# Nine fillers between the M units, w_in's last quarter scaled in one step, six bias additions moved to VectorE

## The chip, the cores and the metric

The program runs on one core of one Trainium2 chip. The core has five engines with instruction streams of their own: TensorE (PE: matmuls, with its weight loads as PEld), VectorE (DVE), ScalarE (ACT), GpSimd (POOL) and SyncE (SP, which here only issues transfers). They meet through semaphores. Matmul results land in PSUM; the other tiles lie in SBUF; large tensors and two scratch arrays lie in DRAM. The metric is the time of one execution on the device in microseconds (us), smaller is better. The kernel before takes 903.31 us, the median of three runs (903.01 to 904.61).

## The reference

Two stages follow each other. The first is a spectral filter over the sequence axis of x, with 8 batches of 3008 positions and 256 channels:

```python
X = np.fft.rfft(x, axis=1);  Xr, Xi = X.real, X.imag
Yr = Xr @ w_r - Xi @ w_i + b_r
Yi = Xr @ w_i + Xi @ w_r + b_i
Yr = np.sign(Yr) * np.maximum(np.abs(Yr) - 0.01, 0.0)   # Yi likewise
y = np.fft.irfft(Yr + 1j * Yi, n=3008, axis=1)
```

The second is a feed-forward layer on all 24064 rows of y, with 2048 hidden features and an ELU between two matrix products:

```python
h = y @ w_in
g = np.where(h > 0.0, h, np.exp(np.minimum(h, 0.0)) - 1.0)
out = g @ w_out
```

## The kernel before

**The transform as matmuls.** 3008 is 47 x 64, so the transform and its inverse are each split into two small ones, and a batch passes through five kinds of units, each a handful of matmuls with one eviction out of PSUM:

- A (`unit_A`, six per batch): 64-point transform of x. ScalarE evicts to the tile A, and pairs of units are stored to the DRAM scratch DA (line 172).
- X (`unit_X`, eight): 47-point transform. Its operand Z is DA read back with another axis on the partitions (`load_Z`, line 181, two transfers). Result: XT.
- M (`unit_M`, twelve): the complex product with the weights, the bias and the soft threshold for 128 frequencies at a time, see below. Result: Y.
- B (`unit_B`, six): first part of the inverse. ScalarE evicts to Bz, and pairs of units are stored to the DRAM scratch DB (line 336).
- Y (`unit_Y`, eight): second part of the inverse. Its operand Bs is DB read back (`load_Bs`, line 344, four transfers). Result: yT, which is the hidden layer's input, transposed.

**The M unit.** The complex product is done with three real products. Xd is the real part minus the imaginary part (GpSimd, line 240, issued two units ahead). One product K = Xd @ w_i goes to one half of the PSUM tile (`kp`), and X_r @ (w_r - w_i) and X_i @ (w_r + w_i) go to the other (`ps[:, 0]`); K added to each gives both parts. VectorE first makes Kb = K + b_r (line 265, 128x256) and then yb = ps + Kb with Kb used for both halves (line 266, 128x512). The imaginary half should have had b_i, so GpSimd adds b_i - b_r (`bias_d`) to that half (line 274, 128x256), then clips (line 275) and subtracts (line 278): the soft threshold.

**The steps.** The feed-forward layer runs in 376 steps, 47 per batch; eight steps make a block of 512 rows, with 256 hidden features per step. `front_mm` (line 789) makes the two halves of the hidden tile `hps` on TensorE. `Elu` then runs over ScalarE, GpSimd or VectorE (lines 803 to 814), and VectorE's mix (line 824) writes `gT`, which also sets the PSUM of `hps` free. `back` (line 844) multiplies by w_out two steps later and adds up in PSUM; after the eighth step the block is evicted (line 855) and stored (line 862).

The transform of the next batch is woven into these steps by hand. `plan(b)` makes a list with one entry per step: while the layer runs on batch b, the steps hold the last Y units of batch b, the X, M, B and first Y units of batch b + 1 (entries ("n", 0) and ("n", 1), called n0 and n1 here), and the A units of batch b + 2. A step holds at most one unit, whose matmuls are issued between the two halves of `front_mm`. Y and A units serve as fillers between the M units; `room` says how many fillers may stand there, `cut` behind which M units, and what is left over stands at the end, behind the last B unit. `f1` holds what is issued late in a step: transfers, the first two Xd, and in the first batch also the weight sums (line 228) and the scaling of w_in.

In a step without an M unit GpSimd does both halves of `Elu.least` (line 812). In a step with an M unit ScalarE does that work in another form, so that GpSimd is free for the M unit's own operations. In the first four steps VectorE does it.

**What sets the order.** Every engine runs its instructions in the order in which the program lists them. All loads and stores of DA, DB, Z, Bs and the outputs are issued by SP in program order, so an instruction of SP that waits for a semaphore holds up those behind it. A unit's PSUM tile has one buffer for all kinds of units (`psF`, line 758), so a unit's matmuls wait until the unit before has been evicted; `hps` has four buffers.

**The last quarter of w_in.** w_in arrives in four quarters and is scaled by 2/3008 into bfloat16 (`scale_w_in`, lines 736 and 738). The last quarter feeds the steps with features 1536 to 2047, of which step 6 is the first; VectorE scales its two halves in steps 4 and 5 of the first batch:

```python
f1[4].append((scale_w_in, (3, True, 0)))
f1[5].append((scale_w_in, (3, True, 1)))
```

Of the kernel before, what the change touches and what calls it, by code (L numbers as in the profile page):

```python
# [8 lines left out]
ALU = mybir.AluOpType  # L9
AF = mybir.ActivationFunctionType  # L10
BF16 = mybir.dt.bfloat16
F32 = mybir.dt.float32
# [13 lines left out]
def kernel(  # L26
# [11 lines left out]
    nc = tc.nc  # L38
    P = nc.NUM_PARTITIONS

    B, S, D = x.shape
# [20 lines left out]
    bias_bc = constp.tile([P, 2 * D], F32, name="bias_bc")  # L62
    bias_d = constp.tile([P, D], F32, name="bias_d")
# [13 lines left out]
    wk1 = ctx.enter_context(tc.tile_pool(name="wk1", bufs=1))  # L77
# [39 lines left out]
    def unit_ps(name, alone):  # L117
        if alone:
            return pre2.tile([P, 2, 512], F32, name=name, tag="pre2")
        return psF.tile([P, 2, 512], F32, name=name, tag="fps")  # L120
# [9 lines left out]
    def later(alone, f):  # L130
        if alone:
            f()
        else:
            after.append(f)
# [99 lines left out]
    def unit_D(b, k):  # L234

        if k >= NJ // 2:
            return
        Xd_of[b, k] = wk3.tile([P, 2, P], BF16, name="Xd", tag="Xd")
        XT, o = XT_of[b], k * P
        nc.gpsimd.tensor_tensor(  # L240
            Xd_of[b, k][:], XT[:, :, 0, o : o + P], XT[:, :, 1, o : o + P], ALU.subtract
        )

    def unit_M(b, q, i):

        k = 2 * q + i
        XT, Xd, o = XT_of[b], Xd_of.pop((b, k)), k * P
        ps = unit_ps("mps", False)
        kp = ps[:, 1, 0:D]
        for lhs, rhs, dst in (  # L250
            (lambda dt: Xd[:, dt], lambda dt: wcat_r[:, dt, D : 2 * D], kp),
            (lambda dt: XT[:, dt, 0, o : o + P], lambda dt: wsum[:, 0, dt], ps[:, 0, 0:D]),
            (lambda dt: XT[:, dt, 1, o : o + P], lambda dt: wsum[:, 1, dt], ps[:, 0, D : 2 * D]),
        ):
            for dt in range(2):
                nc.tensor.matmul(dst, lhsT=lhs(dt), rhs=rhs(dt), start=dt == 0, stop=dt == 1)  # L256
        if i == 0:
            Y_of[b, q] = wk3.tile([P, 2, 2 * D], BF16, name="Y", tag="Y")
        yb = wk3.tile([P, 2 * D], F32, name="yb", tag="yb")
        Y_ = Y_of[b, q]  # L260

        def done():
            two = lambda t: t.rearrange("p (c d) -> p c d", c=2)
            Kb = wk1.tile([P, D], F32, name="Kb", tag="Kb")
            nc.vector.tensor_tensor(Kb[:], kp, bias_bc[:, 0:D], ALU.add)  # L265
            nc.vector.tensor_tensor(  # L266
                two(yb[:]), two(ps[:, 0]), Kb[:].unsqueeze(1).to_broadcast([P, 2, D]), ALU.add
            )

        clips = []  # L270

        def clip_():
            clips.append(wk2.tile([P, 2 * D], F32, name="clip", tag="clip"))
            nc.gpsimd.tensor_tensor(yb[:, D : 2 * D], yb[:, D : 2 * D], bias_d[:], ALU.add)  # L274
            nc.gpsimd.tensor_scalar(clips[0][:], yb[:], LAM, -LAM, ALU.min, ALU.max)  # L275

        def sub_():
            nc.gpsimd.tensor_tensor(Y_[:, i, :], yb[:], clips[0][:], ALU.subtract)  # L278

        jobs.append((clip_, lambda: unit_D(b, k + 2), sub_))  # L280
        later(False, done)

    held = []
# [584 lines left out]
    def put(kind, b, *a):  # L868
        return ({"A": unit_A, "X": unit_X, "M": unit_M, "B": unit_B, "Y": unit_Y}[kind], (b, *a))

    def plan(b):

        f0 = [[] for _ in range(PER)]
        f1 = [[] for _ in range(PER)]
        n1, n2 = b + 1, b + 2
        lead = int(b == 0)
        early = 6 if b == 0 else 4
        seq = [("y", u) for u in range(2, early)]
        if b == 0:
            seq.insert(2, ("-",))  # L880
        rest_ = []
        if n1 < B:
            due = 38 + b
            seq += [("X", u) for u in range(8)]
            fill = [("y", u) for u in range(early, 8)]
            if n2 < B:
                fill += [("A", u) for u in range(6)]
            else:
                fill += [("-",)] * 6
            room = max(0, min(10, due - 5 - (b > 0) - lead - len(seq) - 17))  # L890
            fill, rest_ = fill[:room], fill[room:]
            cut = ([-1, 4] if b == 0 else [-1, 11, 0, 4, 8, 2, 6, 10, 1, 11])[: len(fill)]
            fill = fill[::-1]
            seq += [fill.pop() for c in cut if c < 0]
            for k in range(12):
                seq.append(("M", k // 2, k % 2))
                if k % 2 and k > 1:
                    seq.append(("B", k // 2 - 1))
                for c in cut:
                    if c == k:  # L900
                        seq.append(fill.pop())
            if b == 0:
                seq.append(rest_.pop(0))
            seq.append(("B", 5))
            k = due - lead - len(seq)
            seq += rest_[:k] + [("-",)] * (k - len(rest_))
            seq += [("n", 0), ("n", 1)] + rest_[k:]
        else:
            seq += [("y", u) for u in range(early, 8)]
        xs = (14, 18, 22) if b == 0 else (1, 4, 7)  # L910
        for t, u in enumerate(seq, lead):
            if u[0] == "y":
                f0[t].append(put("Y", b, u[1]))
            elif u[0] == "n":
                f0[t].append(put("Y", n1, u[1]))
            elif u[0] == "A":
                if n2 < B:
                    f0[t].append(put("A", n2, u[1]))
            elif u[0] == "M":
                f0[t].append((unit_M, (n1, *u[1:])))  # L920
            elif u[0] != "-":
                f0[t].append(put(u[0], n1, *u[1:]))
            if u == ("X", 7):
                for k in range(2):
                    f1[t + 1].append((unit_D, (n1, k)))
            if u == ("B", 5):
                f1[t + (0 if b == 0 else 1)] += [(load_Bs, (n1, w)) for w in range(4)]
            if u == ("A", 5) and n2 < B:
                f1[t] += [(load_Z, (n2, s0, s1)) for s0, s1 in ((0, 8), (8, NS))]
        if b == 0:  # L930
            f1[5].append((weight_sum, (0,)))
            f1[6].append((weight_sum, (1,)))
            f1[7].append((weight_sum, (2,)))
            f1[4].append((scale_w_in, (3, True, 0)))
            f1[5].append((scale_w_in, (3, True, 1)))
        if n2 < B:
            for ci in range(3):
                f1[xs[ci]].append((load_x, (n2, ci)))
        return f0, f1
# [5 lines left out]
    for i in range(n + LAG):  # L945
        split = False
        if i < n:
            r = i % PER
            if r == 0:
                f0, f1 = plan(i // PER)  # L950
                used = [bool(u0 or u1) for u0, u1 in zip(f0, f1)]
                kinds = ["M" if any(f is unit_M for f, a in f0[k]) else "F" for k in range(PER)]
# [76 lines left out]
```

## Time and profile before

| what | value |
|---|---|
| median of three runs | 903.31 us (903.01 to 904.61) |
| profiled execution | 905.58 us, of which the span from the first to the last instruction is 903.8 us |
| mean granted TensorE clock | 0.993 of full speed |
| busy share of the span | PE 97%, PEld 74%, DVE 73%, ACT 78%, POOL 73% |
| transferred | 106.32 MB in 90677 packets |

The profile is of one execution. A group row has line, engine, operation, output and inputs with shapes and the count, then busy time and mean ns of one, then the idle time of that engine just before, with what ended it. A row of the timeline has start, length, engine, line, operation, tiles and count, and in brackets the idle time before it with the releaser; consecutive instructions of a kind are merged, and the length is then of the group. SPq is the stretch in which SP issues a transfer, not the transfer itself. In the chain of work that ended last, a DMA row is the time from the issue to what it released. Matmul rows overlap, since they are pipelined.

### The profile page before, as it was taken

The page shows a single profiled execution, that of the slowest core. Times are in us where ns is not written, and L with a number is a line of the kernel's source. Part 1 is how long each engine was busy: PE and PEld are TensorE (multiplying, and loading weights), DVE is VectorE, ACT ScalarE, POOL GpSimd, SP SyncE. Part 2 cuts the span into 40 slices and gives each one's busy share as a digit, 9 for nine tenths or more (in the row PEclk, how much of TensorE's full clock was granted, in tenths as well). Part 3 has the DMA queues.
Part 4 walks back from the last instruction along what each step waited for, and adds up shares of the span by engine and source line. Part 5 has one row for each costly group of instructions (what it writes and reads, how often), then busy time and mean ns, then how long its engine had stood idle before and what let it go on. Part 6 is the DMA issues. An engine that isn't in the chain of part 4 may idle for free.

```text
span 903.8 us, 18245 instructions
## 1 busy us (share of the span) xinstructions
PE 875.0 (97%) x6779; PEld 668.0 (74%) x6889; DVE 655.4 (73%) x1066; ACT 709.3 (78%) x1132; POOL 663.8 (73%) x996
## 2 busy tenths in 40 slices
PE   8888999999999999999999999999997999999997
PEld 3447677787778777887779777788775877778776
DVE  8766776677776777668776777767774677777775
ACT  6667788788887888788887888788885888777664
POOL 6706996679956898669876798668984589866664
PEclk9999999999999999999999999999998999999999
DMA  8992335631285113750247323662227011141011
GB/s 264 356 258 65 117 119 163 188 117 48 61 228 166 61 48 109 219 165 24 83 131 208 117 55 92 167 187 86 71 71 209 25 42 53 48 118 48 25 46 47
DMA packets 90677, 106.32 MB, mean 118 GB/s; under 512 B 5270, under 2 KB 81308, under 8 KB 87228
## 3 DMA queue, kind: packets, MB, share of 16 engines
q1 hardware_dynamic: 84332, 77.62, 30.5%
q0 software_dynamic: 5968, 27.26, 9.7%
q8 instruction: 54, 0.88, 0.4%
q14 instruction: 35, 0.29, 0.1%
q10 hardware_dynamic: 288, 0.26, 0.1%
HBM read 55.32 MB, written 49.81 MB: 116 GB/s over the span
## 4 chain that ended last, share of the span: by engine, by line
PE 84%; DMA 5%; POOL 4%; DVE 3%; ACT 2%; issue 2%; SPq 1%; ACTq 0%; DVEq 0%; POOLq 0%
PE ps_o L844 36%; PE hps L789 31%; PE mps L256 6%; PE bps L314 3%; PE aps L158 2%; PE xps L192 2%; PE yps L355 2%; PE mps L209 1%; DMA w_in_f<-in_moe_w_in_dram 1%; DMA DB<-Bz 1%; POOL Y L278 1%; DMA DA<-A 1%; DMA xt<-in_x_dram 1%; POOL yb L274 1%; POOL Et L812 1%
## 5 line engine op out<-in xcount | busy, mean ns | idle before, releaser
L824 DVE SCALAR_TENSOR_TENSOR gT<-Et,hps 128x512 fp32r<-128x512 f32 x752 | 496.2, 684 | 183.8 <-POOL Et L812 157.0
L812 POOL TENSOR_SCALAR Et<-Et 128x512 f32<-128x512 f32 x576 | 350.2, 615 | 199.3 <-ACT Et L807 197.6
L844 PE MATMUL ps_o<-w_out_r,gT 128*128 128x256 f32 x3008 | 478.0, 302 | 1.1 <-ACT osb L855 0.8
L844 PEld LDWEIGHTS ps_o<-w_out_r,gT 128*128 128x128 f32 x3008 | 404.3, 189 | 53.3 <-ACT osb L855 5.3
L789 PE MATMUL hps<-yT,w_in_s 128*128 128x512 bf16 (+7 forms) x1623 | 419.5, 355 | 4.7 <-DVE gT L824 1.7
L807 ACT ACTIVATE Et<-hps 128x512 f32<-128x512 f32 x584 | 341.5, 603 | 100.7 <-PE hps L789 97.6
L789 PEld LDWEIGHTS <-w_in_s 128*128 128x128 bf16 x1728 | 119.0, 98 | 61.0 <-issue 23.2
L803 ACT ACTIVATE Et<-hps 128x512 f32<-128x512 f32 x168 | 100.6, 599 | 53.2 <-PE hps L789 47.9
L278 POOL TENSOR_TENSOR Y<-yb,clip 128x512 bf16<-128x512 f32 x84 | 108.3, 1289 | 0.3
L805 ACT ACTIVATE Et<-Et 128x1024 f32<-128x1024 f32 x84 | 88.9, 1058 | 2.7
L274 POOL TENSOR_TENSOR yb<-yb,bias_d 128x256 f32<-128x256 f32 x84 | 61.6, 733 | 14.3 <-DVE yb L266 13.1
L266 DVE TENSOR_TENSOR yb<-mps,Kb 128x512 f32<-128x512 f32 x84 | 58.1, 691 | 3.0
L265 DVE TENSOR_TENSOR Kb<-mps,bias_bc 128x256 f32<-128x256 f32 x84 | 35.5, 422 | 33.5 <-PE mps L256 33.3
L275 POOL TENSOR_SCALAR clip<-yb 128x512 f32<-128x512 f32 x84 | 51.5, 613 | 7.4
L240 POOL TENSOR_TENSOR Xd<-XT 128x256 bf16<-128x256 bf16 x84 | 56.2, 672 | 0.0
L126 ACT CAST yT<-yps 128x752 bf16<-128x752 f32 x63 | 49.2, 781 | 8.3 <-PE yps L355 8.2
L126 ACT CAST A<-aps 128x1024 bf16<-128x1024 f32 x45 | 45.4, 1011 | 8.2 <-PE aps L158 7.0
L126 ACT CAST XT<-xps 128x768 bf16<-128x768 f32 x61 | 48.5, 795 | 3.0 <-PE xps L192 3.0
L256 PE MATMUL mps<-wsum,XT 128*128 128x256 bf16 x336 | 50.4, 273 | 0.0
L328 ACT CAST Bz<-bps 128x1024 bf16<-128x1024 f32 x46 | 46.3, 1007 | 0.4 <-PE bps L314 0.4
L355 PEld LDWEIGHTS <-Bs 96*128 96x128 bf16 x512 | 28.9, 100 | 22.2 <-DMA Bs<-DB 8.4
L355 PE MATMUL yps<-M,Bs 96*128 96x94 bf16 x512 | 32.7, 210 | 8.1 <-DMA Bs<-DB 7.0
(116 smaller groups left out, 479.5 us busy)
## 6 DMA issues: line engine op xcount, KB each, us to landing
xt<-in_x_dram POOLq DMA_DIRECT2D x21, 1024.0 KB, 5.4
out_dram<-osb SPq DMA_DIRECT2D x158, 128.0 KB
Bs<-DB SPq DMA_DIRECT2D x32, 384.0 KB
DA<-A SPq DMA_DIRECT2D x21, 512.0 KB
DB<-Bz SPq DMA_DIRECT2D x21, 512.0 KB
Z<-DA SPq DMA_DIRECT2D x7, 1152.0 KB
Z<-DA SPq DMA_DIRECT2D x11, 384.0 KB
xt<-in_x_dram POOLq DMA_DIRECT2D x6, 512.0 KB, 6.1
```

Of the source, the lines that this page charges most:

```text
L126: nc.scalar.copy(dst, src)
L256: nc.tensor.matmul(dst, lhsT=lhs(dt), rhs=rhs(dt), start=dt == 0, stop=dt == 1)
L274: nc.gpsimd.tensor_tensor(yb[:, D : 2 * D], yb[:, D : 2 * D], bias_d[:], ALU.add)
L278: nc.gpsimd.tensor_tensor(Y_[:, i, :], yb[:], clips[0][:], ALU.subtract)
L355: nc.tensor.matmul(psv[:, j, 0 : 2 * N1], lhsT=Bs[:, j, dt * P : dt * P + P], rhs=M4[:], start=True, stop=True,)
L789: nc.tensor.matmul(hps[s][:, c0:c1], lhsT=w_in_s[:, dt, ft * P : ft * P + P], rhs=yT_of[b][:, dt, t0 : t0 + c1 - c0], start=(dt == 0), sto ...
L803: nc.scalar.activation(e, h, AF.Relu, scale=-1.0)
L805: nc.scalar.activation(self.E, self.E, AF.Exp, scale=-1.0)
L807: nc.scalar.activation(e, h, AF.Exp)
L812: nc.gpsimd.tensor_scalar(e, e, 1.0, 0.0, ALU.min, ALU.max)
L824: nc.vector.scalar_tensor_tensor(g_of[self.i][:, p], self.E[:, p], -1.0, self.h[p], ALU.add, ALU.max)
L844: nc.tensor.matmul(po[q][:, i_ % 2, :], lhsT=gT[:, s, i_ * P : i_ * P + P], rhs=w_out_r[:, ft, :], start=(ft == 0 and i_ % 2 == 0), stop=( ...
```

## The change

Three edits. The number of fillers between the M units is limited to nine instead of ten. The second half of w_in's last quarter is scaled in step 4, directly behind the first half. For the six M units with even k of batch 1 (the batch that is prepared during the first batch's steps), VectorE's Kb is made 512 wide, with K repeated and b_r and b_i added to its two halves, so that yb has the right bias in both halves, and GpSimd's addition of `bias_d` is left out. The tile Kb is 512 wide for all M units, and the others use its first half.

```diff
         def done():
             two = lambda t: t.rearrange("p (c d) -> p c d", c=2)
-            Kb = wk1.tile([P, D], F32, name="Kb", tag="Kb")
-            nc.vector.tensor_tensor(Kb[:], kp, bias_bc[:, 0:D], ALU.add)
+            if b == 1 and k % 2 == 0:
+                Kb = wk1.tile([P, 2 * D], F32, name="Kb", tag="Kb")
+                nc.vector.tensor_tensor(
+                    two(Kb[:]), kp.unsqueeze(1).to_broadcast([P, 2, D]), two(bias_bc[:]), ALU.add
+                )
+                nc.vector.tensor_tensor(yb[:], ps[:, 0], Kb[:], ALU.add)
+                return
+            Kb = wk1.tile([P, 2 * D], F32, name="Kb", tag="Kb")[:, 0:D]
+            nc.vector.tensor_tensor(Kb, kp, bias_bc[:, 0:D], ALU.add)
             nc.vector.tensor_tensor(
-                two(yb[:]), two(ps[:, 0]), Kb[:].unsqueeze(1).to_broadcast([P, 2, D]), ALU.add
+                two(yb[:]), two(ps[:, 0]), Kb.unsqueeze(1).to_broadcast([P, 2, D]), ALU.add
             )
...
         def clip_():
             clips.append(wk2.tile([P, 2 * D], F32, name="clip", tag="clip"))
-            nc.gpsimd.tensor_tensor(yb[:, D : 2 * D], yb[:, D : 2 * D], bias_d[:], ALU.add)
+            if not (b == 1 and k % 2 == 0):
+                nc.gpsimd.tensor_tensor(yb[:, D : 2 * D], yb[:, D : 2 * D], bias_d[:], ALU.add)
...
-            room = max(0, min(10, due - 5 - (b > 0) - lead - len(seq) - 17))
+            room = max(0, min(9, due - 5 - (b > 0) - lead - len(seq) - 17))
...
             f1[4].append((scale_w_in, (3, True, 0)))
-            f1[5].append((scale_w_in, (3, True, 1)))
+            f1[4].append((scale_w_in, (3, True, 1)))
```

## The prediction

> **What bounds the kernel now.** I read the page's busy times first, then the 20 us windows, then the waits of TensorE, and only then the timeline at each place where TensorE stands.
>
> ```profile
> span 903.8 us, 18245 instructions
> PE 875.0 (97%) x6779; PEld 668.0 (74%) x6889; DVE 655.4 (73%) x1066; ACT 709.3 (78%) x1132; POOL 663.8 (73%) x996
> ```
>
> TensorE is busy for 875.0 of 903.8 us and the other four rows stay below 80%. An edit that touches no matmul, as this one, can only win what lies in TensorE's 28.8 us of gaps. So the question is which gaps it reaches.
>
> ```profile
> 100.00:120.00 20.00, 18.17 (x139) 13.78 (x141) 14.34 (x25) 15.97 (x24) 19.58 (x27) 1.00 0.50 153
> ...
> 680.00:700.00 20.00, 14.74 (x95) 11.17 (x95) 9.71 (x16) 9.04 (x17) 7.95 (x14) 0.83 0.82 222
> ```
>
> The columns are the stretch, its length, then busy time of PE, PEld, DVE, ACT and POOL, the granted clock and the DMA share. Two stretches stand out, and a part of the change belongs to each: 100 to 120 us, where POOL is busy for 19.58 of 20 us (the first batch's M units), and 680 to 700 us, where everything stands and even the clock falls to 0.83. The third part, the scaling of w_in, lies in the start, near 70 us.
>
> **Part 1, nine fillers at most.** Working the list in `plan` through by hand, `room` exceeds 9 only for b = 5 and b = 6; every other list is unchanged. In b = 5 the tail M11, B4, A4, A5, B5 (steps 33 to 37) becomes M11, B4, A4, B5, A5. For b = 6 the last fillers are empty; B5 moves from step 37 to 36 and no transfer crosses it, while its reader n0 comes at step 44, so that costs and brings nothing. In b = 5 the swap turns the order of SP's queue round. These are its rows for b = 4, whose tail already is B4, A4, B5, A5, and then for b = 5:
>
> ```profile
> 572.85 0.36 SPq L336 DMA_DIRECT2D DB<-Bz  x1
> 575.27 0.36 SPq L172 DMA_DIRECT2D DA<-A  x1
> 576.10 2.30 SPq L344 DMA_DIRECT2D Bs<-DB  x4
> 578.77 0.87 SPq L181 DMA_DIRECT2D Z<-DA  x2
> ...
> 681.41 0.80 SPq L181 DMA_DIRECT2D Z<-DA  x2
> 682.30 0.38 SPq L336 DMA_DIRECT2D DB<-Bz  x1
> 691.25 1.71 SPq L344 DMA_DIRECT2D Bs<-DB  x4
> ```
>
> In b = 5 the two large reads Z go out first, and the store DB that B5 feeds goes out behind them; in b = 4 the store goes first and Bs is being issued 3.25 us later. The chain that ended last shows what the other order costs:
>
> ```profile
> 682.30 8.93 DMA DB<-Bz
> 691.25 4.21 DMA Bs<-DB
> 695.50 0.81 PE yps L355 x8
> ```
>
> The store takes 8.93 us beside Z, and Y unit 0 of the next batch (n0) finds its operand late. TensorE, again b = 4 and then b = 5, each from n0's first hidden matmul to the first one two steps on:
>
> ```profile
> 582.59 0.61 PE L789 MATMUL hps<-yT,w_in_s 128*128 128x512 bf16 x2
> ...
> 586.87 1.05 PE L789 MATMUL hps<-yT,w_in_s 128*128 128x192 bf16 x8
> ...
> 689.69 0.61 PE L789 MATMUL hps<-yT,w_in_s 128*128 128x512 bf16 x2
> 695.50 0.81 PE L355 MATMUL yps<-M,Bs 96*128 96x94 bf16 x8 [5.21 <-DMA Bs<-DB]
> ...
> 701.46 1.05 PE L789 MATMUL hps<-yT,w_in_s 128*128 128x128 bf16 x8
> ```
>
> The same two steps take 4.28 us in b = 4 and 11.77 us in b = 5, 7.49 us more. Of these 5.21 us are the wait; the other 2.28 us come behind it, where the granted clock is half:
>
> ```profile
> 698.00:700.00 2.00, 2.00 (x13) 0.50 0.82 273
> 700.00:702.00 2.00, 2.00 (x21) 1.00 0.03 11
> ```
>
> The Trainium skill (TensorE: Matmul & The Clock Gate, Part 1: The HAM clock gate) puts the half clock down to an idle window of about 3.4 us and lets it last until about 3.4 us have been busy. By that rule the slow matmuls would cost an estimated 1.7 us and the whole term 6.9; the rows' 2.3 us are taken here.
>
> Does the new order end the wait? B5 takes A5's place in step 36 (A5's matmul 676.17). Its operand is the last Y of M11, which POOL finishes at 675.94:
>
> ```profile
> 674.65 1.29 POOL L278 TENSOR_TENSOR Y<-yb,clip 128x512 bf16<-128x512 f32 x1
> ...
> 676.17 0.82 PE L158 MATMUL aps<-xt,M 128*128 128x512 f32 x2
> ```
>
> So B5 starts 0.2 us or more behind that, without a wait. In b = 4 n0 comes six steps after B5, and the store went out 9.7 us before n0's first matmul (572.85 to 582.59). In b = 5 n0 comes seven steps after, so the store would go out 9.7 us and a step (about 2.1 us, half of the 4.28) before 689.69, near 678, on a queue that is not waiting. With b = 4's 3.25 us Bs is issued from about 681.2, 8.5 us ahead of n0; in b = 4 it was 6.5 us ahead and nothing waited. A5's store DA is now queued ahead of the four Bs on SP, and Z behind them: Z goes out near 684, some 2 us later than now, and its reader, X0 of the next batch, comes four steps behind 701.46, near 710 us. A loss would need Z to be late there (third rival). What is queued behind these on SP are output stores, as in b = 4. Term: 7.5 us gained, because b = 4 is the same order with one step less; the ends are 0 (the wait only changes its cause) and 7.5.
>
> **Part 2, w_in's last quarter in step 4.** VectorE scales a half at the end of step 4 and, now, the other at the end of step 5; step 6 needs both.
>
> ```profile
> 48.85 0.68 DVE L736 TENSOR_SCALAR w_in_s<-w_in_f 128x1024 bf16<-128x1024 f32 x1
> ...
> 68.66 1.16 POOL L228 TENSOR_TENSOR wsum<-wcat_r 128x512 bf16<-128x512 bf16 x1
> ...
> 69.06 1.04 DVE L736 TENSOR_SCALAR w_in_s<-w_in_f 128x512 bf16<-128x512 f32 x1 [1.25 <-DMA w_in_f<-in_moe_w_in_dram]
> 69.79 1.36 POOL L812 TENSOR_SCALAR Et<-Et 128x512 f32<-128x512 f32 x2
> 70.02 1.27 DVE L824 SCALAR_TENSOR_TENSOR gT<-Et,hps 128x512 fp32r<-128x512 f32 x2
> 70.75 0.38 PE L789 MATMUL hps<-yT,w_in_s 128*128 128x512 bf16 x1 [0.74 <-DVE gT L824]
> 71.22 1.33 DVE L736 TENSOR_SCALAR w_in_s<-w_in_f 128x512 bf16<-128x512 f32 x1
> 72.60 0.39 PE L789 MATMUL hps<-yT,w_in_s 128*128 128x512 bf16 x1 [1.48 <-DVE w_in_s L736]
> ```
>
> Step 6's first matmul starts at 70.75, its second only at 72.60, behind the second scaling. Moved, that scaling runs from about 70.05, ahead of the pair gT, and everything behind it on VectorE (gT of step 4, which frees the PSUM of step 6) is late by its length. The first half took 1.04 us but ended 0.28 us behind POOL's wsum (69.82). If it costs 0.34 us (half of the 0.68 of the row twice as wide), gT's first half ends near 71.1 and the second matmul starts near 71.4: 1.2 us gained. If it waits until POOL's pair is through (71.15), the matmul starts near 72.4: 0.2 us gained. If it waits for the first of the pair alone, about 72.0 on the same count: 0.7 us, my value, between the ends. The Trainium skill (SBUF — State Buffer, SBUF: two separate sides) calls the port pair of VectorE and GpSimd an exclusive lock held for a whole instruction. The end of the first half 0.28 us behind POOL's instruction agrees.
>
> **Part 3, six bias additions on VectorE.** For M0, M2, M4, M6, M8 and M10 of the first batch POOL loses one 128x256 addition, and VectorE's Kb grows to 128x512. No row shows that Kb; the nearest is yb, as wide and also from PSUM.
>
> ```profile
> L274 POOL TENSOR_TENSOR yb<-yb,bias_d 128x256 f32<-128x256 f32 x84 | 61.6, 733 | 14.3 <-DVE yb L266 13.1
> L266 DVE TENSOR_TENSOR yb<-mps,Kb 128x512 f32<-128x512 f32 x84 | 58.1, 691 | 3.0
> L265 DVE TENSOR_TENSOR Kb<-mps,bias_bc 128x256 f32<-128x256 f32 x84 | 35.5, 422 | 33.5 <-PE mps L256 33.3
> ```
>
> POOL saves 733 ns and VectorE pays 691 - 422 = 269 ns for each. Both can be on the path, since one PSUM buffer serves all units: the next unit waits for yb.
>
> ```profile
> 95.00 0.38 PE L256 MATMUL mps<-wcat_r,Xd 128*128 128x256 bf16 x2 [0.22 <-DVE yb L266]
> ...
> 97.47 0.38 PE L256 MATMUL mps<-wcat_r,Xd 128*128 128x256 bf16 x2
> ...
> 100.32 0.39 PE L256 MATMUL mps<-wcat_r,Xd 128*128 128x256 bf16 x2 [0.44 <-POOL Xd L240]
> ...
> 105.26 0.38 PE L256 MATMUL mps<-wcat_r,Xd 128*128 128x256 bf16 x2
> ...
> 107.39 0.69 DVE L824 SCALAR_TENSOR_TENSOR gT<-Et,hps 128x512 fp32r<-128x512 f32 x1 [2.77 <-POOL Et L812]
> ...
> 109.19 0.51 PE L355 MATMUL yps<-M,Bs 96*128 96x94 bf16 x8 [0.69 <-DVE yb L266]
> ```
>
> M1 starts at 95.00 on M0's yb, so it becomes 0.27 later. M1 to M2 takes 2.47 us without a wait, M2 to M3 2.85: M3 stood 0.38 us for POOL. With POOL 0.5 us earlier that wait goes, but M2's own wider Kb holds M3 to about 100.4, so M3 is 0.1 us late. M4 to Y unit 7 takes 3.93 us instead of 2.47, 1.46 too long, and POOL is the cause by way of gT. POOL gets there earlier by two additions less M0's 0.27: 1.2 us. M4's Kb takes back 0.27, so Y unit 7 comes 0.9 us earlier. Behind it TensorE shows no wait of this kind; there POOL's saving leads VectorE's 0.27. Term: 0.9 us gained. Ends: six Kb on the path and no relief, 1.6 us lost; all of 1.46 + 0.38 and M1's 0.4 gone, 2.2 us gained.
>
> **The sum.** 7.5 + 0.7 + 0.9 = 9.1 us, against the profiled execution's 905.58 us (span 903.8 and 1.78 around it): 896.5. That execution lies 2.27 us above the median of 903.31, and above all three runs. If the 2.27 us lie outside the stall, the median becomes 894.2; if the stall is that much shorter in unprofiled runs, 896.5. I take 895.2, about half way.
>
> **Rivals.**
> First: VectorE becomes the bound in the first batch and part 3 ends at its loss of 1.6 us. M1's wait on yb speaks for it, POOL's 19.58 us against it. 7.5 + 0.7 - 1.6 = 6.6 us, 897.7 on the same half-way count.
> Second, the change doesn't do what it says: Bs is late all the same, now behind A5's DA on the queue. For it speaks that DA was followed in b = 5 by this very stall; against it b = 4, where this order left no wait with one step less. Left is 0.7 + 0.9 = 1.6 us, 901.7 counted from the median, as the stall then stays in both.
> Third, slower: Z, now behind Bs, is late for X0 of batch 6. X0 would be due near 710 - 9.1 = 701 us; Z is issued near 684. It decides from a landing past 712 us, 28 us after its issue (9.1 us used up, and 1.8 more): 905.2 or above. In b = 4 Z was issued at 578.77 in the same order and nothing waited, which speaks against it.
>
> **How the numbers follow.** Forecast 0.82, first rival 0.10, second 0.05, third 0.03. The range reaches from the median less all upper ends (903.31 - 7.5 - 1.2 - 2.2 = 892.4) to the first rival counted from the profiled run (905.58 - 6.6 = 899.0), cut to 892.5 and 898.8; it leaves out the last two rivals and little else. Some 0.2% (1.8 us) is what a measurement here tells from no change; so forecast and first rival are faster, the second is the same, the third slower: 0.92, 0.05, 0.03.
>
> **What would show it.** Right: no wait of yps on Bs near 690 us, the granted clock at 1.00 there, SP's order DB, DA, Bs, Z in b = 5 as in b = 4; the second scaling directly behind the first and step 6's matmuls together; six Kb of 128x512 near 0.69 us and 78 POOL additions instead of 84; Y unit 7 of the first batch less than 3.93 us behind M4. Wrong: yps waiting on DMA again, or X0 on Z in batch 6; M units of the first batch further apart than now, waiting on yb.

## The result and the profile after

The changed kernel takes 895.39 us (median of four runs, 893.78 to 897.26) against 903.47 us before: a ratio of 0.9909 with a 95% interval of 0.9886 to 0.9933, or 8.1 us less (6.1 to 10.3). A second set of five runs (e9) gave 895.92 us and 0.9913 (0.9890 to 0.9936).

The page and the 20 us windows of the profiled execution (columns as before):

```profile
span 892.0 us, 18350 instructions
PE 875.0 (98%) x6889; PEld 665.5 (75%) x6889; DVE 656.0 (74%) x1066; ACT 708.6 (79%) x1132; POOL 659.6 (74%) x990
```

```profile
100.00:120.00 20.00, 19.73 (x154) 14.67 (x155) 16.60 (x28) 16.97 (x26) 18.85 (x26) 1.00 0.48 158
680.00:700.00 20.00, 20.00 (x185) 16.73 (x184) 14.19 (x22) 14.75 (x27) 12.28 (x21) 1.00 0.76 203
```

TensorE's busy time reads 875.0 us as before, but the two figures can't be set against each other: the trace of before holds only 6779 of the 6889 matmuls. From 680 to 700 us it is busy throughout at the full clock (14.74 us and 0.83 before), and from 100 to 120 us for 19.73 us (18.17 before). This profiled execution, at 893.78 us, is the fastest of the four runs, and the one of before, at 905.58 us, was above all of its timed runs. So the 11.8 us between the two spans overstate the gain.

**The tail of b = 5.** SP's queue and, below it, TensorE:

```profile
673.89 0.37 SPq L344 DMA_DIRECT2D DB<-Bz  x1
676.31 0.36 SPq L172 DMA_DIRECT2D DA<-A  x1
677.15 2.26 SPq L352 DMA_DIRECT2D Bs<-DB  x4
679.77 0.79 SPq L181 DMA_DIRECT2D Z<-DA  x2
```

```profile
685.43 0.61 PE L797 MATMUL hps<-yT,w_in_s 128*128 128x512 bf16 x2
685.88 0.50 PE L363 MATMUL yps<-M,Bs 96*128 96x94 bf16 x8
...
689.71 1.05 PE L797 MATMUL hps<-yT,w_in_s 128*128 128x128 bf16 x8
```

The store goes out first, Bs follows 3.26 us later, then Z. n0's Y matmul starts 0.45 us behind the hidden matmul, without a wait, and the two steps take 4.28 us instead of 11.77.

**The start.** VectorE with GpSimd and TensorE, from the timeline:

```profile
67.29 1.18 DVE L744 TENSOR_SCALAR w_in_s<-w_in_f 128x512 bf16<-128x512 f32 x2
...
68.39 1.27 DVE L832 SCALAR_TENSOR_TENSOR gT<-Et,hps 128x512 fp32r<-128x512 f32 x2
...
69.32 0.60 PE L797 MATMUL hps<-yT,w_in_s 128*128 128x512 bf16 x2
...
69.76 0.51 PE L192 MATMUL xps<-M,Z 96*128 96x96 bf16 x8
```

The two scalings run directly behind each other, and step 6's two matmuls too. VectorE doesn't wait for the transfer, which had landed by 67.29, 0.33 us ahead of Y unit 5; in the trace of before it landed at 69.05, 0.9 us behind it. From Y unit 5 to X unit 0 it is 2.14 us, the length of a step, instead of 4.67.

**The first batch's M units.** Of each unit the first matmul row, M0 to Y unit 7:

```profile
89.08 0.38 PE L256 MATMUL mps<-wcat_r,Xd 128*128 128x256 bf16 x2
...
92.19 0.38 PE L256 MATMUL mps<-wcat_r,Xd 128*128 128x256 bf16 x2 [0.49 <-DVE yb L269]
...
94.67 0.38 PE L256 MATMUL mps<-wcat_r,Xd 128*128 128x256 bf16 x2
...
97.36 0.38 PE L256 MATMUL mps<-wcat_r,Xd 128*128 128x256 bf16 x2
...
100.19 0.61 PE L322 MATMUL bps<-Y,M 64*128 64x256 bf16 x8 [0.19 <-DVE yb L273]
...
102.57 0.38 PE L256 MATMUL mps<-wcat_r,Xd 128*128 128x256 bf16 x2
...
105.04 0.51 PE L363 MATMUL yps<-M,Bs 96*128 96x94 bf16 x8
```

and the groups of the two new forms, with the one that got fewer:

```profile
L282 POOL TENSOR_TENSOR yb<-yb,bias_d 128x256 f32<-128x256 f32 x78 | 57.1, 732 | 13.5 <-DVE yb L273 12.3
...
L269 DVE TENSOR_TENSOR yb<-mps,Kb 128x512 f32<-128x512 f32 x6 | 4.1, 691 | 0.2
L266 DVE TENSOR_TENSOR Kb<-mps,bias_bc 128x512 f32<-128x512 f32 x6 | 4.1, 687 | 1.9 <-PE mps L256 1.9
```

The wide Kb takes 687 ns. M0 to M1 is 3.11 us now (2.86 before), and M1 waits for M0's yb; M4 to Y unit 7 is 2.47 us (3.93 before), which is the length of such a step without a wait.

### The profile page after: what moved, and what is told of

It is laid out like the page before. It is cut to its first block, busy times and chain, and to the rows that moved or that the text cites. A ratio compares the mean times of both kernels' runs of the same rounds, so it can differ in the third digit from the quotient of the medians.

```text
span 892.0 us, 18350 instructions
## 1 busy us (share of the span) xinstructions
PE 875.0 (98%) x6889; PEld 665.5 (75%) x6889; DVE 656.0 (74%) x1066; ACT 708.6 (79%) x1132; POOL 659.6 (74%) x990
## 4 chain that ended last, share of the span: by engine, by line
PE 90%; DMA 4%; POOL 2%; ACT 1%; issue 1%; DVE 1%; SPq 0%; ACTq 0%; POOLq 0%
PE ps_o L852 38%; PE hps L797 36%; PE mps L256 6%; PE bps L322 3%; PE xps L192 2%; PE yps L363 2%; PE aps L158 2%; DMA DA<-A 1%; PE mps L209 1%; DMA Z<-DA 1%; DMA xt<-in_x_dram 1%; DMA Bs<-DB 0%; POOL Y L286 0%; ACT Et L811 0%; POOL xt L115 0%
## 5 line engine op out<-in xcount | busy, mean ns | idle before, releaser
L797 PE MATMUL hps<-yT,w_in_s 128*128 128x512 bf16 (+4 forms) x1728 | 438.1, 354 | 1.4 <-DVE gT L832 0.6
L282 POOL TENSOR_TENSOR yb<-yb,bias_d 128x256 f32<-128x256 f32 x78 | 57.1, 732 | 13.5 <-DVE yb L273 12.3
L272 DVE TENSOR_TENSOR Kb<-mps,bias_bc 128x256 f32<-128x256 f32 x78 | 33.0, 423 | 34.4 <-PE mps L256 34.2
L273 DVE TENSOR_TENSOR yb<-mps,Kb 128x512 f32<-128x512 f32 x78 | 53.9, 691 | 2.7
L192 PEld LDWEIGHTS <-Z 96*128 96x128 bf16 x512 | 28.7, 98 | 15.9 <-DMA Z<-DA 3.4
```

What stands on the lines that cost most here:

```text
L797: nc.tensor.matmul(hps[s][:, c0:c1], lhsT=w_in_s[:, dt, ft * P : ft * P + P], rhs=yT_of[b][:, dt, t0 : t0 + c1 - c0], start=(dt == 0), sto ...
```

## Experiments

The table holds, for every kernel that ran, three stretches between the starts of TensorE's units (from the timelines) and the median of the timed runs (one run where marked). y5 to X0 (Y unit 5 to X unit 0) is what part 2 touches, M0 to A0 (18 steps) part 3, A3 to n0 the first batch's wait for Bs. The first column is where the scaling of w_in's last quarter began, counted from the start of Y unit 5. Where it is negative, VectorE didn't wait for the transfer, except in e1; where it is positive, and in e1, it is the landing.

| kernel | scaling behind y5 | y5 to X0 | M0 to A0 | A3 to n0 | median, us |
|---|---|---|---|---|---|
| before | 0.90 | 4.67 | 46.78 | 3.04 | 903.47 |
| after | -0.33 | 2.14 | 45.40 | 3.63 | 895.39 |
| e1, nine only | -0.09 | 2.51 | 46.87 | 3.29 | 895.98 |
| e2, scaling only | -0.45 | 2.14 | 46.83 | 3.56 | 903.34 |
| e3, bias only | 0.56 | 4.68 | 45.43 | 3.10 | 902.09 |
| e4, Z later | 0.09 | 2.98 | 46.79 | 3.97 | 895.87 |
| e5, late quarter | 4.83 | 7.05 | 45.41 | 3.69 | 903.10 (one) |
| e6, odd M | -0.46 | 2.14 | 45.05 | 3.69 | 892.82 (one) |
| e7, all M | -0.45 | 2.14 | 45.71 | 3.51 | 894.13 (one) |
| e8, early x, split store | -0.60 | 2.14 | 44.63 | 2.48 | 893.02 |
| e9, after again | 0.13 | 3.20 | 45.40 | 3.25 | 895.92 |
| e10, M0 alone | 0.22 | 3.20 | 44.68 | 2.48 | 893.50 |
| e11, no wide Kb | 0.29 | 3.20 | 45.21 | 2.48 | 895.62 (one) |
| e12, e8 again | -0.47 | 2.14 | 44.63 | 2.68 | 892.22 |

The kernel before ran beside e1 to e4 at 903.93 us and beside e9 to e12 at 903.06 us.

### e1 to e3: each part alone

```diff
-            room = max(0, min(10, due - 5 - (b > 0) - lead - len(seq) - 17))
+            room = max(0, min(9, due - 5 - (b > 0) - lead - len(seq) - 17))
```

> Only the limit of nine fillers; the other two parts as before. Theory (the stall of b = 5 is worth 5.2 us of waiting and 2.3 us of half clock, and the swap of A5 and B5 ends it): the profile shows no wait of yps on Bs near 690 us, n0's two steps take 4.3 us instead of 11.8, and the time falls by 6 to 7.5 us, to 896 to 897.5. Rival (the wait only changes its cause): n0 still waits, time within 1 us of before. From the difference of the two sums, if parts 2 and 3 bring what the trace of after shows (2.5 and 1.1 us), this run should stand above after by up to 3.6 us; if they bring nothing outside that one profile, it equals after.

Measured: 895.98 us, a ratio of 0.9906 (0.9879 to 0.9934), 8.5 us less. No wait of yps near 690 us. This one line alone reads as much as all three parts together (8.1 us), so the timed runs don't show that the other two add to it.

```diff
-            f1[5].append((scale_w_in, (3, True, 1)))
+            f1[4].append((scale_w_in, (3, True, 1)))
```

> Only the scaling of w_in's last quarter in step 4; the rest as before. Theory as predicted: 0.7 us gained (0.2 to 1.2), about 902.7. Rival, from the trace of after, where the second matmul of step 6 no longer stood at all: the quarter lands at a different time in each execution, and with an early landing both scalings fit ahead of GpSimd's sums; then step 6's unit starts some 2.5 us earlier against step 5's and the time is near 901.0. In the profile: first scaling starts at 67.3 (early landing, VectorE does not wait for the transfer) or near 69.1 (late landing); the stall of b = 5 stays.

Measured: 0.9993 (0.9975 to 1.0011), between 1.0 us slower and 2.3 us faster, so both sizes are allowed by the time. The trace was one of an early landing: the first scaling starts at 67.47, y5 to X0 is 2.14 us. Across the profiles without this part that stretch is 4.67, 2.51, 4.68 and 2.98 us, with it (e5 left aside) 2.14 six times and 3.20 three times. The means are 3.7 and 2.5, but their difference of 1.2 us is not the part's worth: by the table the six short ones had the quarter early and the two of 4.7 late, and no landing occurred early without the part or, e5 aside, as late with it.

```diff
+            if b == 1 and k % 2 == 0:
...
-            nc.gpsimd.tensor_tensor(yb[:, D : 2 * D], yb[:, D : 2 * D], bias_d[:], ALU.add)
+            if not (b == 1 and k % 2 == 0):
+                nc.gpsimd.tensor_tensor(yb[:, D : 2 * D], yb[:, D : 2 * D], bias_d[:], ALU.add)
```

> Only the six wider Kb, with GpSimd's six additions left out; the rest as before. Theory: M1 0.27 us later after M0 than before (3.1 us instead of 2.86), M4 to Y unit 7 about 2.5 to 3.0 us instead of 3.93, in all 0.9 to 1.4 us gained by step 31, time near 902.4. Rival (VectorE is the bound): M units further apart all through, the stretch from M0 to A0 (46.8 us before) unchanged or up to 1.6 us longer, time 903.5 to 905.1.

Measured: 0.9975 (0.9960 to 0.9990), 0.9 to 3.6 us less. M0 to A0 is 45.43 us against 46.78 to 46.87 without the part: 1.4 us, the same to a tenth in every profile with the part. It is made of M0 to M1 +0.26, M2 to M3 -0.14, M3 to B0 +0.25, M4 to Y unit 7 -1.46 and M10 to M11 -0.31. VectorE does take some back, but it is not the bound.

### e4: the order on SP's queue, or the distance

Both B5's place and the order of the queue change in part 1. This one keeps B5 in step 37 and moves only Z:

```diff
             if u == ("A", 5) and n2 < B:
-                f1[t] += [(load_Z, (n2, s0, s1)) for s0, s1 in ((0, 8), (8, NS))]
+                f1[t + (3 if b == 5 else 0)] += [(load_Z, (n2, s0, s1)) for s0, s1 in ((0, 8), (8, NS))]
```

> Ten fillers as before, so B5 of b = 5 stays in step 37, six steps ahead of n0; only the two reads Z of b = 5 are issued three steps later, behind the four Bs. Theory (SP's order, Z ahead of the store DB, is the cause): the store lands in about 3 us, Bs is issued within 4 us of it, no wait at n0, the same gain as with nine fillers, 896 to 897.5. Rival (the cause is that B5 stands too few steps ahead of n0, and the swap helps because it gives a seventh step): the wait stays, several us long, and the time stays within 2 us of before.

Measured: 895.87 us, 0.9900 (0.9876 to 0.9924). SP's queue and TensorE's n0:

```profile
678.80 0.36 SPq L336 DMA_DIRECT2D DB<-Bz  x1
682.04 1.74 SPq L344 DMA_DIRECT2D Bs<-DB  x4
...
687.42 2.23 SPq L181 DMA_DIRECT2D Z<-DA  x2
```

```profile
688.04 0.61 PE L789 MATMUL hps<-yT,w_in_s 128*128 128x512 bf16 x2
688.49 0.50 PE L355 MATMUL yps<-M,Bs 96*128 96x94 bf16 x8
```

Bs is issued 3.24 us behind the store and n0 doesn't wait, six steps after B5. So it is the order that costs: a store of 512 KB that a chain waits for, queued behind two reads of 1.5 MB for which there was time. The step won by the swap isn't needed.

The cost has two parts. In e4 the store went out 0.03 us behind the end of ScalarE's B5 eviction (678.77). In the trace of before that eviction ended at 680.41, but SP stood until 681.41 at the first Z, whose operand DA had not landed, and the store went out at 682.30: 1.9 us in the queue. From its issue to that of Bs it then took 8.95 us instead of 3.24, 5.7 us more. Whether these 5.7 us are shared bandwidth or order inside the queue no run here separates.

### e5 and e9: a late landing

```diff
-    load_w_in(3)
     scale_w_in(2, False)
     for s0, s1 in ((0, 8), (8, NS)):
         load_Z(1, s0, s1)
+    load_w_in(3)
```

> The changed kernel, but the transfer of w_in's last quarter is issued behind the two reads Z, so that it lands late: the case for which the prediction sized part 2. From the start of the first scaling to X unit 0 the kernel before took 3.77 us. Theory as predicted (GpSimd holds up the second scaling once): 0.7 us less, about 3.1 us. Bounds of the prediction: 3.6 us if the second scaling waits for both of GpSimd's operations, 2.5 us if it runs straight behind the first. Rival (the gain seen in the trace of after comes from the early landing alone): 3.77 us or more even with both scalings in one step.

Measured: 2.22 us from the first scaling (74.41) to X unit 0 (76.63), less than the lower bound. The edit overshot: the quarter landed so late that GpSimd had run out of work, so that the two scalings took 0.76 us together, and the case of the prediction wasn't met. The late landing and the half clock behind it also explain most of the run's 903.10 us: X unit 2 comes 7.0 us later behind Y unit 5 than in after. e9, the changed kernel once more, came nearer by itself:

> The changed kernel once more, beside e10 and e11 on one chip. As before: 893.5 to 897 us, M0 to A0 45.4 us, M0 to M1 3.1 us. The interval from y5 to X unit 0 is 2.14 us in this profile too, if part 2 covers every landing of w_in's last quarter up to that of the kernel before; with a landing as late as 69 us it would be near 3.

VectorE, GpSimd and TensorE of e9, from the timeline:

```profile
66.96 0.61 POOL L820 TENSOR_SCALAR Et<-Et 128x512 f32<-128x512 f32 x1 [0.57 <-ACT Et L815]
67.17 1.98 DVE L744 TENSOR_SCALAR w_in_s<-w_in_f 128x512 bf16<-128x512 f32 x2 [0.49 <-DMA w_in_f<-in_moe_w_in_dram]
...
67.54 1.34 POOL L228 TENSOR_TENSOR wsum<-wcat_r 128x512 bf16<-128x512 bf16 x1
...
69.81 0.59 PE L797 MATMUL hps<-yT,w_in_s 128*128 128x512 bf16 x2 [0.91 <-DVE gT L832]
...
70.24 0.51 PE L192 MATMUL xps<-M,Z 96*128 96x96 bf16 x8
```

VectorE waits for the landing, and from the first scaling to X unit 0 it takes 3.07 us; the prediction's count was 3.77 - 0.7. The pair of scalings takes 1.98 us instead of 0.76. The first takes 0.68 us of it and ends at 67.85, 0.28 us behind GpSimd's Et (67.57); the second ends at 69.15, 0.27 us behind GpSimd's sum (68.88). That fits the exclusive lock of the Trainium skill (SBUF — State Buffer, SBUF: two separate sides): each scaling waits for one whole instruction of GpSimd, as the prediction assumed. But it is not quite its case: here the quarter landed 0.13 us behind Y unit 5, there 0.90, and other instructions of GpSimd hold the scalings. That the two counts agree to the hundredth is luck (e10 has 2.98, e11 2.91).

At such a landing the part gains nothing. e4, without part 2, had the quarter 0.09 us behind Y unit 5:

```profile
67.53 0.72 DVE L736 TENSOR_SCALAR w_in_s<-w_in_f 128x512 bf16<-128x512 f32 x1 [0.42 <-DMA w_in_f<-in_moe_w_in_dram]
...
69.36 0.77 DVE L736 TENSOR_SCALAR w_in_s<-w_in_f 128x512 bf16<-128x512 f32 x1
...
70.42 0.51 PE L192 MATMUL xps<-M,Z 96*128 96x96 bf16 x8
```

With the scalings a step apart y5 to X0 is 2.98 us, with both in step 4 it is 3.20 in e9, e10 and e11: the mix gT of step 4 goes ahead of the second scaling in e4, and in e9 it waits behind it.

### e6 and e7: which M units

The condition `k % 2 == 0` becomes `k % 2 == 1` in e6 and is left out in e7.

> The changed kernel with the wide Kb on M1, M3, M5, M7, M9 and M11 instead of the even ones: as many additions off GpSimd, but in other places. Theory (a wide Kb costs 0.27 us only where the next unit waits for yb): M0 to M1 goes back from 3.11 to 2.86 us, M1 to M2 from 2.48 to at most 2.6, M3 to B0 gets up to 0.27 longer than 2.83, M4 to Y unit 7 stays near 2.5; M0 to A0 45.2 to 45.7 us (after 45.40). Rival (it is GpSimd's relief before M3 that counts, and odd places give it later): M2 to M3 back to 2.85 and M4 to Y unit 7 above 3 us, M0 to A0 46 us or more.

Measured: M0 to M1 2.85, M1 to M2 2.52, M2 to M3 2.49, M3 to B0 2.99, M4 to Y unit 7 2.46; M0 to A0 45.05 us, 0.35 better than the even units and just below the range expected.

> The changed kernel with the wide Kb on all twelve M units of the first batch. Theory (GpSimd's backlog is gone with six already, and VectorE's 0.27 us is on the path where one unit waits for the other's yb): M0 to A0 stays or gets longer, 45.4 to 46.2 us. Rival (GpSimd is still the bound): M0 to A0 gets shorter by another 0.5 us or more, to 44.9 or below.

Measured: 45.71 us, 0.31 worse than with six. M3 to B0 is 3.10 us, and the row of B0 in its timeline says why:

```profile
100.20 0.61 PE L322 MATMUL bps<-Y,M 64*128 64x256 bf16 x8 [0.48 <-DVE yb L269]
```

With all twelve additions moved M3's Kb is wide as well, and its 0.27 us are on the path to B0; nothing shows a further gain from GpSimd.

### e8, e10 to e12: beyond the change

In the trace of after, two gaps of the first batch remain that the change doesn't treat: GpSimd issues a load of x in step 14, ahead of work that holds up M0's yb and so M1, and n0 waits 0.99 us for Bs.

```diff
-            if alone:
+            if alone or (b == 1 and v >= 4):
                 k0 = 4 * v
...
-        xs = (14, 18, 22) if b == 0 else (1, 4, 7)
+        xs = (8, 10, 12) if b == 0 else (1, 4, 7)
```

> A version beyond the change: the changed kernel, with the three loads of x that GpSimd issues in steps 14, 18 and 22 of the first batch issued in steps 8, 10 and 12, and the last store DB of the first batch split in two halves, so that B4's half goes out a step and more earlier. Theory: without its 0.65 us issue in step 14 GpSimd frees gT of that step earlier, so M0 to M1 falls from 3.11 us to 2.5; and the wait of n0 on Bs near 147 us (A3 to n0 3.63 us) shrinks by 0.6 to 1.1 us; together 1.2 to 1.8 us below after, 893.5 to 895 in the timed runs. Rival (the issue of x lies beside other work, and Bs is late for another reason than the size of the store): both intervals unchanged, time as after.

Measured: 893.02 us, 0.9875 (0.9854 to 0.9896) of before. M0 to M1 is 2.47 us and A3 to n0 2.48, both without a wait; together they give 1.8 us against after, as expected, and the time is just below the range.

> e8 once more, on the chip of e9 and e10. 1.2 to 2.4 us below e9 (M0 to A0 0.8 us shorter, A3 to n0 1.1 us shorter); the rest of the difference, either way, is the start, where the landing of the first transfers differs between executions.

Measured: 892.22 us (891.29 to 893.50), 0.9874 (0.9851 to 0.9897) of before; all its runs lie below all runs of e9 on the same chip (894.53 to 896.85). The medians are 3.7 us apart, more than the 1.2 to 2.4 expected: M0 to A0 gives 0.8 us, A3 to n0 0.6 in this pair, and an earlier landing of w_in's last quarter 1.1 that are not the edit's. M0 and M1, and n0 with the two half stores ahead of it:

```profile
88.37 0.38 PE L256 MATMUL mps<-wcat_r,Xd 128*128 128x256 bf16 x2
...
90.84 0.38 PE L256 MATMUL mps<-wcat_r,Xd 128*128 128x256 bf16 x2
...
145.04 0.51 PE L363 MATMUL yps<-M,Bs 96*128 96x94 bf16 x8
```

```profile
132.63 0.37 SPq L339 DMA_DIRECT2D DB<-Bz  x1
...
138.14 0.55 SPq L339 DMA_DIRECT2D DB<-Bz  x1
140.79 1.75 SPq L352 DMA_DIRECT2D Bs<-DB  x4
```

The second half lands within 2.65 us; Bs follows 3.56 us behind the whole store in after.

With GpSimd relieved in this way, are the wide Kb still needed?

> e8 with the wide Kb on M0 alone. Theory (with the x loads issued early GpSimd has 1.3 us more ahead of M4, so that the addition left out at M0 is enough, and each further wide Kb only costs its 0.27 us where yb is waited for, as at M2 to M3 and M3 to B0): M2 to M3 falls from 2.71 to 2.5, M3 to B0 from 2.83 to 2.6, M4 to Y unit 7 stays at 2.5 to 2.7, M0 to A0 44.1 to 44.5 us (e8 44.63). Rival (GpSimd's backlog comes back): M4 to Y unit 7 above 2.9 us, M0 to A0 44.9 or more.

Measured: 893.50 us, 0.9888 (0.9866 to 0.9911). M2 to M3 falls to 2.47 as expected, but M3 to B0 stays at 2.81 and M4 to Y unit 7 is 2.64; M0 to A0 44.68 us, as in e8 (44.63) and not the 44.1 to 44.5 expected. One wide Kb does what six did: the 0.24 us won from M2 to M3 are lost again behind it.

> e8 with no wide Kb at all: part 3 taken back, with the early x loads and the split store kept. Theory: the early x loads alone give GpSimd 1.3 us of the 1.5 that Y unit 7 stood for; M4 to Y unit 7 2.5 to 3.0 us, M0 to M1 2.5, M0 to A0 44.3 to 45.0 us. Rival (only the additions matter): M4 to Y unit 7 near 3.9 us again, M0 to A0 46 us or more.

Measured: M4 to Y unit 7 3.18 us, M0 to A0 45.21 us, both some 0.2 above the ranges expected and well below the rival's. The early loads alone bring 1.6 of the 46.8 us, the wide Kb 0.5 to 0.6 more.

## Why the prediction was right, point by point

**What bounds the kernel** held in the main: TensorE's waits had to go, and they went. That only the 28.8 us of gaps could be won was too narrow, though. The 2.3 us at half clock, which the prediction counted as part of the term, are busy time. The equal 875.0 us hide this, since the trace of before misses records. The busy times of e9, the kernel of after with 111 matmul records missing, and of e2, with none missing and the stall still there, are:

```profile
PE 869.7 (97%) x6778; PEld 665.5 (74%) x6889; DVE 657.5 (74%) x1066; ACT 708.6 (79%) x1132; POOL 660.1 (74%) x990
PE 879.3 (98%) x6889; PEld 667.5 (74%) x6889; DVE 653.9 (73%) x1066; ACT 709.8 (79%) x1132; POOL 665.5 (74%) x996
```

In the complete traces TensorE is busy for 878.2 to 879.3 us with the stall (e3, e2) and 875.0 to 877.3 without (after, e1, e4).

**Part 1** held in its mechanism and in its place. e1 gives its size alone, 8.5 us (6.0 to 10.9), and e4 shows the cause that was given: Z ahead of the store. The rival that Bs is late all the same is refuted by both; the slower rival (Z late for X unit 0) by the trace of after, where X unit 0 follows its neighbours by a step's 2.14 us. The 7.49 us were those of one execution. From B5 to the third Y unit behind it, it took 26.80 us in the trace of before, 25.57 in e2 and 26.14 in e3, which have the same order, and 19.30 in e4: 7.5, 6.3 and 6.8 us more than in e4. The profile of before was the worst of the three: it waited 5.21 us and worked for 4.5 us at half clock, e2 4.64 and 3.2, e3 4.73 and 4.1. That is the shorter stall for which the prediction went half way to the median.

**Part 2** has no single size, and there the prediction went wrong: it took the landing of w_in's last quarter, 69.05 us in that trace, as a fixed point. The landing differs between executions (landed by 66.5 in e12, at 69.8 in e11), and with it the whole gap. At the one close pair of landings (e4 and e9) the part costs 0.2 us instead of gaining 0.7. Between the earliest landings of the two kinds (e1 and the six of 2.14) it is 0.4 us gained, and at a landing as late as the one assumed, where 4.7 us stood before, no profile has the part with GpSimd still at work. The timed runs of e2 say 0.6 us, between 1.0 lost and 2.3 gained. What did come out is the lock: one instruction of GpSimd for each scaling.

**Part 3** was 1.4 us instead of 0.9. M1's delay (0.27 predicted, 0.25 measured), M3's (0.1 and 0.1) and the wide Kb's length (691 ns taken, 687 measured) came out. Y unit 7 came 1.1 us earlier against M0, not 0.9. Of its 1.46 us all went, since the 0.27 us that M4's wide Kb was to take back didn't show: Y unit 7 starts without a wait. Two items were missing: B0 starts 0.25 us later behind M3, on whose yb it waits, since VectorE has the block's eviction and two mixes to do between M2's yb and M3's Kb, and a wait of 0.3 us between M10 and M11 went too. "Behind it TensorE shows no wait of this kind" was wrong there. The rival that VectorE becomes the bound is refuted for six units, and comes true in part for twelve (e7).

**The sum.** From the profiles part 1 is 6.9 us on average and part 3 is 1.4; with e2's 0.6 for part 2 that is 8.9 us, close to the 9.1 forecast, and the timed runs say 8.1 (6.1 to 10.3). That the median came within 0.2 us of the forecast 895.2 is partly luck: part 1 was 0.6 us too large, part 3 half a us too small, part 2 belongs to a landing that did not come again, and the way half back to the median was a choice between two values. The three parts alone sum to 8.5 + 0.6 + 2.3 = 11.4 us by the timed runs, with intervals of 1.4 to 2.5 us to either side. So the timed runs do not tell whether something is lost when the parts stand together; the intervals of the units show no such loss.

## What to carry to other kernels

Before timing a wait on a transfer, read the issuing queue in order around it: here 7 us hung on which of two transfers was listed first, the first of them not even ready yet, and a sister stage of the same program with the other order gave the price of the repair. Where several executions can be had, take a wait on a transfer from all of them, since it differs by microseconds where engine work repeats within a tenth, and compare kernels only at like landings. And when an engine is overloaded in one stretch, look first for what can be done earlier (the x loads, 1.6 us) before work is moved to a neighbour that has to be waited for as well (the wide Kb, 0.5 us on top).

## What was not expected

Stretches bound by engines repeat from execution to execution and chip to chip: M0 to A0 is 45.40, 45.41 and 45.40 us in after, e5 (which differs only in the start) and e9. The start doesn't: the time of Y unit 5 goes from 66.25 (e3) to 70.02 us (e8). In the two profiles of e8's kernel X unit 0 is 3.1 us apart, and the runs differ by 2.8; in the two of the changed kernel it is 0.5 of 1.5, so the start is not all.

The stall before cost TensorE 2.3 us beyond its 5.2 us through the half clock. In e5, too, the 4.4 us wait of step 6 was followed by a slow step: X unit 0 to X unit 1 took 4.08 us instead of 2.14. The granted clock stood at 0.50 for 6.8 us each in before (693.2 to 700.0), e3 (690.1 to 696.9) and e5 (74.2 to 81.0), and for 3.4 us, half of that, in e2 (692.9 to 696.3), so the same stall costs more in one execution than in another. A shorter wait, the 0.99 us at n0 of the first batch in after, left the clock at 1.00.
